# Six late skip terms seeded into PSUM by VectorE, with rows of x loaded into freed memory, and a new step list

## The chip, the cores and the metric

The kernel runs on one core of a Trainium2 chip. The metric is the device time of one execution in microseconds (us), taken as the median of several runs. A profile of one execution gives the spans and rows quoted here. The engines are named as the profile names them: PE (TensorE matmul), PEld (its weight loads), DVE (VectorE), ACT (ScalarE), POOL (GpSimd), and SP, whose queue issues most of the DMAs.

## The reference

The input x is 2048 x 512 in bfloat16. Two branches are computed from it and mixed by a gate.

```python
g = sigmoid((x * gate_w).sum(-1, keepdims=True))
# branch a: a diagonal complex state-space model and a skip term
Lam_bar = exp(dt * Lam);  B_bar = ((Lam_bar - 1) / Lam)[:, None] * Bmat
Bu = einsum("bld,pd->blp", x, B_bar)
h_t = Lam_bar * h_{t-1} + Bu_t                       # over 2048 rows
a = 2 * einsum("blp,dp->bld", hseq, Cmat).real + x * Dskip
# branch b: linear attention, 32 heads of 16, no causal mask
q, k, v = split(x @ wqkv)
phi(u) = concat(softmax(u @ w_phi), softmax(-(u @ w_phi)))
b = ((phi(q) @ kv) / (phi(q) @ z + 1e-6)) @ wo       # kv, z summed over all rows
out = g * a + (1 - g) * b
```

The change concerns the skip term `x * Dskip` of six of the sixteen output tiles.

## The kernel before, in words

The 2048 rows are handled as 16 tiles of 128 rows. Tile `ti` holds the rows with residue `ti // 2` modulo 8, in one half `ti % 2`, so that the recurrence can be run on eight residues with a scan over 128 blocks. The last stages run over the tiles in the order `order[n]`, n = 0 to 15.

All work of PE, DVE, ACT and the SP queue is put down in one hand-ordered string, `ORDER`. Each word of it is one step of a generator: `y8@6` advances the generator `st_y(8)` by one step and gives it PSUM bank 6, `o5:D` lets DVE do a copy that ACT would do otherwise, `t9:A` issues a DMA on ACT's queue in place of SP's. Every engine executes its own instructions strictly in the order in which the words stand, so an instruction that waits holds up all later ones of its engine.

The words that matter here:

- `F:34` issues 34 small matmuls without use (`spin`), ahead of the transposes `W0` to `W3` of the key weights and their folding `f0` to `f3`.
- `k`, `u`, `v` and `q` are the projections of a tile. `x`, `n`, `e` and `s` (capital letters behind the word `END`) are the feature maps: maximum, minimum, exponentials and normalisation of a group of four tiles. The last steps of `S1`, `S2` and `S3` multiply by a ratio on DVE (line 572) and issue four DMA transposes on SP (line 584), which give `phT`.
- `g`, `z`, `Z` and `h` are the state-space part, `c` the products that form the output matrices.
- `END` closes the memory pools of the first part and opens those of the second in their place.
- `y{n}` opens PSUM tile `py` with eight matmuls of 512 columns (line 754) and then adds the skip term by four matmuls of 128 columns against a diagonal matrix `Dd` (line 759).
- `o{n}` forms the attention numerators from `phT` (line 773), scales them on DVE into `on` (line 781) and transposes them into `oT`. For n = 0 to 11 that is a DMA transpose on SP (line 795), for the last four it is done by PE.
- `t{n}` adds four matmuls with `Wo` to the same `py` (line 802), scales by the gate (ACT line 806 or DVE line 808) and writes the rows out (line 810).

BT (transposes of B) and BD (the block matrix of the feature map) lie in the pool `pAC`, which is closed at `END`. `H_SEED` names eight `h` steps where ACT already writes a PSUM bank before matmuls accumulate onto it.

Of the kernel before, what the change touches and what calls it, by code (L numbers as in the profile page):

```python
# [25 lines left out]
R2 V@7 V U U f3@2 f3 P P P2 P2 P2 k0@4 V2@7 k3@1 P P2 P2 P2 P3 k0 V2 R5 P4 P4 P4 gw i3 k1@0 i1 i0 R3 k2@5 k1 k2 i0 i3  # L26
x0 u1@7 u1 Q1 P3 i3 v3@6 i1 i1 k3 i3:D u3@0 u3 i3 i1:D i1 v3 x0 u2@5 n0 n0 i0 x0 u0@7 x0 C0 u2 i0:D x0 i0 i2 n0 v2@2
x1 k5@4 k5 i2 v2 n0 x1 C6 u5@6 u5 i2 u0 i2:D i2 u4@0 k7@3 L k4@6 n0 U Q0 k4 C2 v4@7 k7 k6@1 k6 n1 u4:D n1 x1 Q2 v1@6
v1 e0 v5@5 e0 v7@0 k10@1 u7@4 v8@2 v5 n1 u8@6 Q3 u7 n1 v6@3 U v7 x1 x1 k10 v4 M v0@4 v0 n1 v6 x2 n2 k9@0 k9 k8@1 k8
u6@5 x2 n2 n2 u6 x2 s0 x2 n2 s0 s0 s0 s0 C3 s0 D k11@3 C4 e1 e1 k12@1 k12 C1 s0 k13@5 g40@7 k13 g00@0 g40 a0@15 a0 g00  # L30
s1 s1 C5 k11 u8 v8 C7 s1 s1 g10@7 g10 g10 g60@3 s1 g20@2 g60 x2 s1 k14@0 n2 k15@4 e2 e2 x3 g20 g30@7 s1 n3 a1 a1 g30
x3 n3 J0 e2 k14 J2 g30 e2 J1 x3 g50@2 g01@3 g50 g50 g01 n3 k15 x3 n3 g70@6 g70 g70 g62@2 x3 g70 n3 e3 g70 g11@4 g11 s2
g62 s2 s2 J3 g61@7 x4 s2 s2 s2 x4 g70:D g21@0 n4 g11 g41@6 x4 g21 g02@3 e3 e3 e3 g22@4 w2@0 w2 g22 s2 a2 g41 g51@2 g02
z0 z0 g61 n4 a2 z0 z0 a2 a2 u11@0 g31@4 n4 u11 z0 z0 n4 w0@6 w0 g31 g31 z0 s3 R7 w1@7 w1 g42@3 g42 z0 s3 x4 g51 g51 s3
s3 s3 z0 z0 Z0@7 s3 g71@0 w3@3 g71 v9@6 w3 q0@2 g71 g71 J2 J3 x4 n4 Z0 h50@3 e4 R6 h10@4 g71 g12@7 q0 g12 s3 h50 q3@2
h10 g71 a3 z1 g12 c4:D e4 e4 e4 h60@3 q3 z1 h60 g32@7 g32 q2@3 q2 g32 z1 v9 q1@4 q1 z1 u10@2 g52@0 g52 z1 z1 c2 g52 J1
g72@4 z1 g72 u10 c3 s4 z1 c5:D g72 g03@7 s4 nA c5 xA s4 g72 g72 g72 xA J0 v11@6 z1 z1 v12@0 s4 c5 nA v12 v13@3 s4 v11
v13 c2:D xA z2 u12@2 z2 u9@4 u9 c2 O v10@0 s4 u14@6 z2 v14@3 z2 z2 z2 u14 g03 g13@4 Z1@7 g13 xA v10 u15@6 c4 z2 g13
u15 nA z2 nA v14 c6:D z2 z2 a3 a3 a3 Z2@4 Z1 g23@0 c4 c6 h11@7 g23 Z2 c0 g33@6 xA nA c0 g33 g33 h52@0 c1 h51@4 u12 eA
h52 h11 g63@3 h12@6 g43@0 g43 g73@2 h62@0 g63 u13@7 g53@3 g53 h51 h61@4 s4 a4 eA eA h62 u13 v15@0 h12 h22@7 g53 eA c0  # L40
h61 h20@6 h22 sA h20 g73 v15 q10@3 a4 g73 h31@7 q10 g73 sA c1 g73 g73 a4 a4 Y h21@0 G q4@4 h31 h21 h31 G c1 q14@6 q14
q5@3 h30@0 Y q8@2 G c3 z3 z3 Y q5 z3 z3 h30 z3 z3 sA h30 z3 z3 c3 Y q8 q11@1 q11 sA sA z3 z3 q6@3 h41@0 sA h32@6 c6
q9@5 Z3@7 h33@1 Z3 q13@2 q4 h41 sA sA h32 q13 q9 sA h53@7 h53 h33 h33 sA h32 c7 q7@4 h13@2 h13 q6 q15@5 q7 q15 c7:D
h01@3 h63@0 h63 h02@0 sA h42@7 h42 c7 h03@5 h40@1 h23@6 h40 y6@2 h23 sA y2@4 h43@7 h01 h43 y6 h03 h00@1 h00 END h02
# [5 lines left out]
y11@1 E3 o8@2 S3 o8 o8@7 o8 o8 o8 o7 y11 S3 S3 o8 o9@2 o9 o9@7 o9 o9 y10 y12@2 o9 o9 y12 S3 t5:A S3 o11@7 S3 o11:D y12  # L50
y11 S3 S3 y10 o10@7 o10 t7 t7:D o11@7 o11 o11 o11 t8 t8:D S3 o11 S3 o10@7 o10 o10 S3@5 S3 o10 o10 t9 t9 S3@7 y15@3
S3:D o12@4 o12:D o12@7 t0 o14@5 o14:D y15 y15 o12 o12 t11 t1:A t11 o12 o14@4 o14 o12@5 o12:D y14@7 o13@5 o13:D t2
o13@1 o13:D o15@4 t8 o14 o14 t4 o13 t10 o15:D y14 o13 y14 o15@1 o14@4 t7:A t11:A o15:D o13@5 t12 o13:D t10 o15 t3 t13
t6:A t10 t12 t12 o15 o14:D t9:A o15@6 t14 t14 o15:D t13:D t13 t15 t15:D t15:A t14
# [18 lines left out]
def kernel(  # L73
# [667 lines left out]

    def phT_of(g):
        def make():
            live["ph", g] = pools["fq"][1].tile([P, 4, NB, P], BF16, name="phT")
            return lambda u: live["ph", g][:, u]
        return make

    def st_y(n):
# [8 lines left out]
        for kt in range(KT):
            xs = xT[:, kt, ti * P:(ti + 1) * P]
            MM(out=py[:, kt * P:(kt + 1) * P], lhsT=xs, rhs=Dd[:, kt, :], start=False, stop=False)
# [38 lines left out]
    def st_t(n):  # L798
        ti = order[n]
        py, oT = live["py", n], live["oT", n]  # L800
        for g in range(HG):
            MM(out=py[:], lhsT=oT[:, g, :], rhs=Wo[:, g, :], start=False, stop=(g == HG - 1))  # L802
        yield
        ot = pools["op"][1].tile([P, D], BF16, name="ot", bufs=14)
        if sel["eng"] == "act":
            nc.scalar.mul(out=ot[:], in_=py[:], mul=G[:, ti:ti + 1])  # L806
        else:
            VS(out=ot[:], in0=py[:], scalar1=G[:, ti:ti + 1], scalar2=None, op0=ALU.mult)
# [76 lines left out]
```

## Time and profile before

| | |
|---|---|
| median of 3 runs | 154.06 us (153.87 to 154.93) |
| profiled execution, its own time | 154.0 us |
| its span, first to last instruction | 151.9 us |
| time outside the span | 2.1 us |
| granted TensorE clock, mean | 0.995 |
| PE busy | 145.0 us, 95% |
| DVE busy | 136.1 us, 90% |
| ACT busy | 127.4 us, 84% |

PE busy includes the latency of pipelined matmuls. A group of four matmuls of 128 columns adds 0.22 us to PE's queue although the mean time of one is given as 219 ns; where PE is full, the distances between starts count. DVE and ACT rows likewise overlap their neighbours by about 0.1 us.

### The profile page before, as it was taken

The numbers are of one execution on the slowest core, as the hardware profiler recorded it, in microseconds if no ns is written. First come the engines' busy times: TensorE is split into PE (matmuls) and PEld (weight loads), VectorE is DVE, ScalarE is ACT, GpSimd is POOL, SyncE is SP. The second block draws the span as 40 slices with busy tenths as digits, with TensorE's granted clock in tenths as the row PEclk, the third lists the DMA queues.
The fourth block names the chain that finished last, engine by engine and source line by source line (L and its number), as shares of the span: only waits on it lengthen the run. The fifth ranks groups of instructions, "written<-read, shape, count | busy, mean of one in ns | idle before, by whom it ended". The sixth has DMA issues, their size and how long they took to land.

```text
span 151.9 us, 3442 instructions
## 1 busy us (share of the span) xinstructions
PE 145.0 (95%) x1251; PEld 99.9 (66%) x1268; DVE 136.1 (90%) x327; ACT 127.4 (84%) x305; POOL 14.7 (10%) x47
## 2 busy tenths in 40 slices
PE   7899999999999999999999999999999999999990
PEld 7647475778989976789887456655444655556640
DVE  3889999999999999999999999999999978874561
ACT  3389999999899999999999999989897759565550
POOL 8246880000000000000000000000000000000000
PEclk9999999999999999999999999999999999999998
DMA  3885997493454698830000003933076669747743
GB/s 104 178 209 81 201 206 152 96 99 85 97 103 100 123 208 175 173 125 4 0 0 4 2 0 76 134 70 69 0 107 140 139 138 155 160 105 172 245 142 104
DMA packets 48737, 17.03 MB, mean 112 GB/s; under 512 B 42064, under 2 KB 48720, under 8 KB 48720
## 3 DMA queue, kind: packets, MB, share of 16 engines
q1 hardware_dynamic: 47008, 15.36, 52.7%
...
q8 instruction: 10, 0.16, 0.5%
...
## 4 chain that ended last, share of the span: by engine, by line
PE 40%; SPq 30%; DVE 14%; DMA 10%; issue 3%; ACT 0%
SPq L236 13%; PE py L802 8%; PE pq L484 7%; PE py L754 7%; SPq L303 6%; DMA oT<-on 6%; PE pgq L619 6%; SPq L295 5%; PE pv L497 3%; SPq L299 3%; PE ph L705 3%; DMA X<-HM 2%; DMA HM<-in_A_C_im_dram 2%; DVE Bn L709 2%; DVE mxq L524 2%
## 5 line engine op out<-in xcount | busy, mean ns | idle before, releaser
L619 PE MATMUL pgq<-xT,BT 128*128 128x256 bf16 x256 | 31.8, 272 | 0.0
L619 PEld LDWEIGHTS <-BT 128*128 128x128 bf16 x256 | 24.7, 98 | 3.3
L143 ACT ACTIVATE EEk<-EEk 128x1024 bf16<-128x1024 bf16 x20 | 20.4, 1065 | 0.0
L484 PEld LDWEIGHTS <-xT 128*128 128x128 bf16 x128 | 12.1, 97 | 11.4 <-DMA xT<-in_A_x_dram 0.5
L124 ACT CAST uv<-pgq 128x512 bf16<-128x512 f32 x28 | 15.9, 594 | 1.1 <-PE pgq L626 0.6
L497 PE MATMUL pv<-Wv,xT 128*128 128x256 bf16 (+1 forms) x128 | 16.1, 272 | 0.0
L802 PE MATMUL py<-Wo,oT 128*128 128x512 bf16 x61 | 15.2, 379 | 0.5 <-DMA oT<-on 0.3
L484 PE MATMUL pq<-Wq,xT 128*128 128x512 bf16 x59 | 15.4, 378 | 0.3
L484 PE MATMUL pk<-Wk,xT 128*128 128x512 bf16 x60 | 15.2, 379 | 0.5 <-DMA xT<-in_A_x_dram 0.3
L497 PEld LDWEIGHTS <-xT 128*128 128x128 bf16 x128 | 12.2, 97 | 3.3 <-issue 0.5
L143 ACT ACTIVATE ld<-pn 128x16 f32<-128x16 f32 x32 | 5.8, 188 | 8.2 <-PE pn L773 7.7
L143 ACT ACTIVATE EEq<-EEq 128x1024 bf16<-128x1024 bf16 x12 | 11.9, 1049 | 0.2 <-DVE EEq L540 0.2
L124 ACT CAST vx<-pv 128x256 bf16<-128x256 f32 x31 | 11.7, 416 | 0.0
L124 ACT CAST Xq<-pk 128x512 bf16<-128x512 f32 x16 | 9.1, 597 | 0.5 <-PE pk L484 0.4
L802 PEld LDWEIGHTS <-oT 128*128 128x128 bf16 x64 | 5.6, 97 | 5.7 <-DMA oT<-on 0.7
L561 DVE TENSOR_TENSOR EEk<-EEk,rck 128x4096 bf16<-128x4096 bf16 (+1 forms) x5 | 9.3, 1857 | 0.0
L773 PEld LDWEIGHTS <-phT 128*128 128x128 bf16 x128 | 6.7, 97 | 3.8 <-issue 0.3
L124 ACT CAST Xq<-pq 128x512 bf16<-128x512 f32 x16 | 9.0, 604 | 0.0
L806 ACT ACTIVATE ot<-py,G 128x512 bf16<-128x512 f32 x9 | 6.2, 687 | 3.3 <-PE py L802 3.3
L524 DVE TENSOR_TENSOR smk<-smk 128x512 bf16<-128x512 bf16 (+4 forms) x18 | 8.1, 450 | 0.3
L608 ACT ACTIVATE phT<-X,dgB 128x512 bf16<-128x512 bf16 x11 | 8.2, 758 | 0.0
L124 ACT CAST nu<-pn 128x256 bf16<-128x256 f32 x22 | 8.1, 379 | 0.0
...
## 6 DMA issues: line engine op xcount, KB each, us to landing
X<-HM SPq DMA_DIRECT2D x8, 256.0 KB, 3.8
...
C2r<-in_B_wqkv_dram ACTq DMA_DIRECT2D x2, 256.0 KB, 3.6
...
```

Of the source, the lines that this page charges most:

```text
L124: nc.scalar.copy(out=out_ap, in_=in_ap)
L143: ins = nc.scalar.activation(**kw)
L236: nc.sync.dma_start_transpose(out=xT[:, :, ti * P:(ti + 1) * P], in_=x_res[ti // 2, ti % 2])
L303: nc.sync.dma_start_transpose(out=CA[:, ri, kt, :], in_=(A_C_re, A_C_im)[ri][:, kt * P:(kt + 1) * P])
L484: MM(out=pt[:], lhsT=xT[:, kt, ti * P:(ti + 1) * P], rhs=W[:, kt, :], start=(kt == 0), stop=(kt == KT - 1))
L497: MM(out=pv[:], lhsT=xT[:, kt, ti * P:(ti + 1) * P], rhs=Wvg[:, kt, c * hd:(c + 1) * hd + c], start=(kt == 0), stop=(kt == KT - 1))
L524: VT(out=dst, in0=cur[:, :, :, 0:n, :], in1=cur[:, :, :, n:2 * n, :], op=op)
L561: VT(out=E5, in0=E5, in1=rc.to_broadcast([P, L, 2 * NB, Dh, 4]), op=ALU.mult)
L608: nc.scalar.mul(out=t_, in_=x_, mul=c_)
L619: MM(out=pg[:, h, :], lhsT=BT[:, kt, 2 * j + h, :], rhs=xT[:, kt, r * NC:(r + 1) * NC], start=(h == 0 and kt == 0), stop=(r % 2 == 0 and k ...
L754: MM(out=py[:], lhsT=hs(r, t, slice(a * P, (a + 1) * P)), rhs=C2B[t], start=(t == 0), stop=False)
L802: MM(out=py[:], lhsT=oT[:, g, :], rhs=Wo[:, g, :], start=False, stop=(g == HG - 1))
```

## The change

For n = 8, 9, 10, 11, 13 and 15, `y{n}` has a new first step: DVE multiplies 128 rows of x, as they lie in memory, by Dskip laid over all partitions, and writes the product in float32 into the PSUM bank `py`. The eight matmuls then accumulate onto it, and the four matmuls against `Dd` are left out. For this, a new step `XN` issues five DMAs on SP: Dskip to 128 partitions (128 KB), and four loads of 256 KB with the rows of x of two tiles each. They go into the memory of BD and BT, which move to the pool `pBC` that stays open to the end. So the pools opened at `END` begin at other memory than before.

```diff
+Y_SEED = (8, 9, 10, 11, 13, 15)
...
-    BD = pAC.tile([P, HG, P], BF16, name="BD")
-    BT = pAC.tile([P, KT, NT2, P], BF16, name="BT")
+    BD = pBC.tile([P, HG, P], BF16, name="BD")
+    BT = pBC.tile([P, KT, NT2, P], BF16, name="BT")
+    xn = BT[:].rearrange("p k t c -> p (k t c)").rearrange("p (n d) -> p n d", n=8)
+    Db = BD[:].rearrange("p k f -> p (k f)")
...
+    def st_XN():
+        nc.sync.dma_start(out=Db, in_=A_Dskip.unsqueeze(0).to_broadcast([P, D]))
+        yield
+        for h in range(4):
+            ti = order[8 + 2 * h]
...
+            nc.sync.dma_start(out=xn[:, 2 * h:2 * h + 2, :], in_=x2.rearrange("(c a r) d -> r c a d", r=NR, c=P)[ti // 2])
+            yield
...
+        if n in Y_SEED:
+            VT(out=py[:], in0=xn[:, n - 8, :], in1=Db, op=ALU.mult)
+            yield
         for t in range(NT2):
-            MM(out=py[:], lhsT=hs(r, t, slice(a * P, (a + 1) * P)), rhs=C2B[t], start=(t == 0), stop=False)
+            MM(out=py[:], lhsT=hs(r, t, slice(a * P, (a + 1) * P)), rhs=C2B[t], start=(t == 0 and n not in Y_SEED), stop=False, skip_group_check=n in Y_SEED)
             if t % 4 == 3:
                 yield
+        if n in Y_SEED:
+            return
         for kt in range(KT):
             xs = xT[:, kt, ti * P:(ti + 1) * P]
```

The step list is new as a whole. What of it the prediction speaks of: the first words, and the stretch in which `S1` ends.

```diff
-B NI l10 l8 F:34 W0@1 W0:D W1@7 W1:D l9 W2@5 W2:D NR W3@2 W3 l11 l12 l13 l14 R0 R1 f0@3 f0:D l15 f1@1 f1 R4 f2@5 f2:D
+NI B l8 NR l12 F:54 W0@5 W0:D l9 W1@4 W1 W3@0 W2@3 W2 W3:D l10 l11 f0@6 f0:D f1@4 f1 f3@5 f3:D l13 f2@2 f2 V@7 V U U P P
...
-S1 N2 S1 o3 S1 q12 t0 y1@0 o1 S1 o3 S1 o1 N2 t0 S1 y8 S1 S1 S1 S1 E2 E2 y9@4 y1 y9 X3 t3 X3 X3 N3 E2 E2 X3 t3 X3 S2 y1
+XN N2 X2 y1@3 y1 y1 N2 X2 S1 o3 XN S1 o3 N2 S1 o1 o1 t0 S1 t0 N2 S1 S1 S1 y4@7 y8@6 S1 S1 S1 S1 X3 S1 y13@5 X3 E2 E2
+y9@2 X3 N3 y8 y8 E2 E2 X3 X3 S2 t3 t3 t3:A t1 t1 y9 o4@4 y13 o4 o4@3 o4 y9 o4 o4 o5@4 o5 o5@3 o5 o5 y13 S2 S2 o6@4 o6
```

The copies change hands too. Ahead of `END`, DVE gives one of its three `W` copies, the copy of `u4` and, on balance, one half product of `c` to ACT. Behind `END` it gives away the copies in `o5`, `o6`, `o7`, `o11`, `o13`, `o14` and `o15` and two scalings (`t8`, `t13`), and takes over one in `o12` and `o14` each, the scaling of `t12` and the copy of one `phT`. Five output DMAs move from SP to ACT's queue and three the other way.

More of the change, by code (lines that the diff above doesn't have):

```diff
@@ L24 @@
 ORDER = """
-B NI l10 l8 F:34 W0@1 W0:D W1@7 W1:D l9 W2@5 W2:D NR W3@2 W3 l11 l12 l13 l14 R0 R1 f0@3 f0:D l15 f1@1 f1 R4 f2@5 f2:D
[L26 to L44, printed above, removed]
@@ L45 @@
-o0@6 X1 h01 h03 y6 h00 y2 N1 o0 o0@1 y5@6 h02 o0 o2@3 o2 o2@1 o2 o2 o0 y2 y5 o1@1 o3@3 y3@5 y3 y3 X1 N1 o1 X1 y0@1 y0
-y0 N1 X1 N1 X1 N1 E1 y5 E1 E1 X2 o2 o2 X2 E1 o1@0 o1 t2 o3 o3@0 o3 N2 o0 o0 X2 o3 q12@7 N2 X2 N2 X2 S1 o1 y8@3 G t2 S1
-S1 N2 S1 o3 S1 q12 t0 y1@0 o1 S1 o3 S1 o1 N2 t0 S1 y8 S1 S1 S1 S1 E2 E2 y9@4 y1 y9 X3 t3 X3 X3 N3 E2 E2 X3 t3 X3 S2 y1
-t1 y4@1 t1 o4@7 o4 o4@5 o4 S2 N3 S2 y13@0 o4 o4 y9 S2 o5@5 o5 o5@7 y8 o5:D o5 o5 S2 S2 y4 o4 N3 o6@7 o6:D o6@5 N3 o6
-y4 y13 o6 o6 o5 o6 S2 S2 S2 y7@5 y7 y7 o7@7 S2 S2 S2 y13 o7 N3 t4 t4:D t5 t5:D o7@7 E3 E3 o7:D E3 t6 y10@6 t6:D o7 o7
@@ L50 @@
[L50 to L54, printed above, removed]
+NI B l8 NR l12 F:54 W0@5 W0:D l9 W1@4 W1 W3@0 W2@3 W2 W3:D l10 l11 f0@6 f0:D f1@4 f1 f3@5 f3:D l13 f2@2 f2 V@7 V U P P
@@ new lines @@
+P R0 P2 P2 P2 P2 U k0@3 k0 R1 V2@0 P2 k1@4 P4 P4 P4 l14 R2 P3 l15 P3 V2 k1 i3 i1 i0 P2 gw i0 i3 i3 i3:D i3 i0 R3 n0
+i0:D i0 k2@2 k2 i1 i1 R5 x0 k3@3 k3 n0 n0 i2 x0 x0 i2 v3@4 v3 u1@6 R4 u1 u2@7 u2 u4@0 u4 v2@5 x0 u5@2 i2 i1:D i1 U v2
+i2:D i2 Q1 k5@1 x0 x1 k5 n0 u3@7 u5 x1 x1 L C0 u3 k7@4 k7 u0@0 u0 k4@1 k4 k6@2 n0 n1 n1 C2 v5@5 x1 u6@3 k6 v7@6 v5 C6
+v1@1 u6 C4 v7 e0 v0@0 v0 U v4@5 M v6@7 n1 v6 e0 v8@4 n1 x1 n1 u7@3 u7 n2 k8@6 k8 k12@7 x2 Q0 v4 k9@6 D k10@0 e1 v1 e1
+k11@1 x2 s0 s0 x2 k13@5 s0 s0 n2 Q2 s0 s1 k10 s0 g40@2 s1 s0 k13 s1 k12 x2 s1 n2 g40 k9 g20@3 g20 a0@72 v8 k11 a0
@@ new lines @@
+g00@0 k14@3 g00 s1 s1 n2 x2 n2 n3 Q3 k14 u8@4 s1 g10@0 g10 x3 x3 u8 g10 k15@1 e2 e2 g30@3 a1 J0 g30 g30 n3 k15 a1
+g50@4 g50 g01@1 x3 e2 e2 g60@5 n3 g50 x3 C7 n3 x3 n3 e3 n4 u11@0 s2 g60 x4 g62@3 s2 g01 g70@4 g70 g02@5 g62 u11 g70
+g70 e3 g70 g41@3 n4 u10@1 g21@6 C1 s2 x4 s2 x4 g02 s2 s2 g70:D g41 n4 C3 g11@0 g11 g22@4 C5 e3 e3 g11 z0 g22 g61@5 n4
+z0 g51@3 x4 z0 z0 z0 g61 z0 J1 w1@0 w1 u10 s2 g21 a2 a2 J2 w0@4 z0 a2 a2 s3 s3 z0 g31@1 g31 s3 w0 s3 s3 s3 g31 w2@5 w2
+z0 z0 g42@0 x4 w3@6 w3 g51 n4 g51 g42 Z0@5 Z0 J2 g71@1 g71 g71 q0@6 h50@0 g71 s3 e4 h10@3 h10 g71 g71 z1 z1 q0 h50
@@ new lines @@
+v9@4 v9 J3 g12@5 a3 g12 g12 J3 q1@1 e4 e4 R6 h60@4 z1 v10@3 e4 v10 q1 z1 z1 z1 h60 q2@0 q2 q3@4 v12@5 z1 q3 z1 c2:D z1
+z1 s4 c5:D g32@6 g32 g32 Z1@3 c3 v12 s4 Z1 g52@1 g52 g52 c4 R7 h11@3 g72@4 J1 xA c5 s4 s4 s4 g72 g72 g03@5 g03 J0
+u14@6 xA nA xA g72 g72 g72 s4 c2:D nA v14@0 v14 u9@5 c2 u9 O h11 g23@1 g23 c4 c5 g13@3 g13 g13 nA z2 nA z2 z2 z2 z2
+u14 v13@4 v11@1 v11 z2 v13 u15@0 xA z2 z2 a3 c4 z2 c0 c6 c0 u15 h51@6 a3 a3 z2 Z2@3 h51 Z2 g43@4 g33@5 g43 u13@3 xA c1
+h52@0 nA h52 c1 c1 g33 c0 g63@6 g33 u13 s4 h61@0 h61 h62@4 g53@5 g63 h12@6 u12@3 eA g53 h62 eA u12 h12 g73@1 v15@3 g53
@@ new lines @@
+eA h20@5 g73 h20 h21@4 v15 G a4 a4 h22@0 g73 c6 g73 h21 eA h22 a4 a4 Y q5@3 c6 G h31@5 Y g73 g73 sA h30@4 q6@0 h31 h31
+q5 Y q6 sA z3 z3 Y q14@7 q10@1 q10 h30 h30 q8@6 q8 sA z3 z3 z3 z3 sA sA h32@0 z3 h41@2 q14 z3 h41 sA sA q9@1 z3 z3
+q13@5 q9 sA sA sA q11@3 h32 q13 G q11 c3 h40@4 Z3@2 Z3 h40 h32 h33@7 sA q4@1 q4 q7@3 q7 c3 h53@5 h53 h42@2 h42 h13@6
+h13 h33 h33 c7 c7:D q15@0 h63@5 h63 y6@1 c7 h00@2 q15 h43@6 h43 sA h01@5 h03@0 h23@3 h02@7 y6 y6 h01 h01 y2@6 h02 h02
+h03 h03 h00 h00 h23 END o0@3 o0 y2 o0@4 o0 y2 o2@7 o2 o2@0 X1 o2 o2 o0 N1 XN X1 o1@2 N1 o1 X1 N1 X1 y0@5 y0 y0 N1 X1
@@ new lines @@
+N1 y3@4 o2 o0 X2 E1 E1 q12@2 y3 o3@3 E1 E1 XN o2 o0 y5@0 o3 o3@7 o3 y5 y5 t2 G o3 o1@7 XN X2 q12 N2 t0 o1 o1 y3 X2 t2
+XN N2 X2 y1@3 y1 y1 N2 X2 S1 o3 XN S1 o3 N2 S1 o1 o1 t0 S1 t0 N2 S1 S1 S1 y4@7 y8@6 S1 S1 S1 S1 X3 S1 y13@5 X3 E2 E2
+y9@2 X3 N3 y8 y8 E2 E2 X3 X3 S2 t3 t3 t3:A t1 t1 y9 o4@4 y13 o4 o4@3 o4 y9 o4 o4 o5@4 o5 o5@3 o5 o5 y13 S2 S2 o6@4 o6
+o5 o4 o5 o6@3 o6 o6 S2 N3 o6 y4 o6 S2 S2 S2 N3 N3 S2 S2 S2 y7@4 S2 S2 N3 o7@3 y7 y7 o7 y4 o7@3 t4 t4:D t1:A t5 y11@7
+o7 o7 o7 o7 E3 t5:D t6 t6:D y11 y11 y10@0 E3 E3 E3 S3 o8@1 o8 o8@3 o8 o8 o8 o8 t4:A S3 y10 y10 o9@1 S3 o9 t5:A y12@3
@@ L55 @@
+o9@1 o9 o9 S3 o9 S3 S3 y12 o11@1 o11 S3 S3 o9 S3 S3 y12 o10@1 o10 t7 o11@1 o11 o11 t7:D t8 t8 o11 y15@6 S3@1 o10@4
+S3:D o10 o10 t9 o10 o11 t9 S3@4 y15 o12@1 t2:A o14@2 S3:D o12 o14 y15 o14@1 o14:D o12@4 o12:D o10 t8 o12 o12 o14 y14@2
+o13@1 o13:D y14 o13@4 o14 o13:D o15@1 o15:D t11 y14 o12@1 o12:D o13 t11 o15@4 o15 t10 o15 t7 o13 o15 t6:A t10 o14@1
+o13@4 t11 o13 o14:D t12 t12:D o15@7 t14 t13 o15 t12:A t14 t13 t13:A t10 t9 t15 t15:D t15:A t14
 """
@@ L740, in st_END @@
         yield
+    def st_XN():
[3 more added lines that the diff above has]
+            ti = order[8 + 2 * h]
+            for a in range(2):
+                assert order[8 + 2 * h + a] == ti + a
+            nc.sync.dma_start(out=xn[:, 2 * h:2 * h + 2, :], in_=x2.rearrange("(c a r) d -> r c a d", r=NR, c=P)[ti // 2])
+            yield
     def phT_of(g):
@@ L801, in st_t @@
         for g in range(HG):
-            MM(out=py[:], lhsT=oT[:, g, :], rhs=Wo[:, g, :], start=False, stop=(g == HG - 1))
+            MM(out=py[:], lhsT=oT[:, g, :], rhs=Wo[:, g, :], start=False, stop=(g == HG - 1), skip_group_check=n in Y_SEED)
         yield
@@ L815 @@
     st = {"V": st_V(), "V2": st_V2(), "U": st_U(), "P": st_P(), "P2": st_P2(), "P3": st_P3(), "P4": st_P4(), "B": st_B(), "gw": st_gw(),
-          "M": st_M(), "D": st_D(), "L": st_L(), "G": st_G(), "Y": st_Y(), "END": st_END(), **{f"Z{j}": st_Z(j) for j in range(4)}, "NR": st_N(0), "NI": st_N(1), "O": st_O()}
+          "M": st_M(), "D": st_D(), "L": st_L(), "G": st_G(), "Y": st_Y(), "END": st_END(), **{f"Z{j}": st_Z(j) for j in range(4)}, "XN": st_XN(), "NR": st_N(0), "NI": st_N(1), "O": st_O()}
     for n in range(8, NTI):
```

## The prediction

> **What bounds the kernel now.** I read the page's busy times first, then a table of busy time by stretch, then PE's and SP's lists of waits, then the order of time around the waits that were left.
>
> ```profile
> PE 145.0 (95%) x1251; PEld 99.9 (66%) x1268; DVE 136.1 (90%) x327; ACT 127.4 (84%) x305; POOL 14.7 (10%) x47
> ```
> ```profile
> core 0: us, PE busy (x) PEld busy (x) DVE busy (x) ACT busy (x) POOL busy (x), PEclk, DMA share, GB/s
> 1.11:9.40 8.29, 7.81 (x76) 5.94 (x78) 5.91 (x32) 4.24 (x7) 4.23 (x13) 1.00 0.71 165
> 9.40:97.20 87.80, 87.04 (x770) 65.91 (x777) 86.40 (x209) 85.63 (x197) 9.95 (x30) 1.00 0.54 102
> 97.20:115.00 17.80, 17.69 (x129) 9.58 (x129) 17.66 (x37) 16.31 (x38) 0.00 (x0) 1.00 0.45 58
> 115.00:123.00 8.00, 7.85 (x72) 4.50 (x72) 7.59 (x16) 4.67 (x17) 0.00 (x0) 1.00 0.67 144
> 123.00:133.30 10.30, 9.86 (x85) 5.45 (x85) 8.27 (x15) 7.97 (x23) 0.00 (x0) 1.00 0.84 154
> 133.30:148.30 15.00, 14.76 (x129) 8.48 (x132) 9.35 (x22) 8.56 (x27) 0.00 (x0) 1.00 0.60 168
> ```
>
> PE is full: between 1.11 and 148.3 it is idle for 0.48 + 0.76 + 0.11 + 0.15 + 0.44 + 0.24 = 2.18 us. But up to 115 us DVE is just as full (86.40 of 87.80, 17.66 of 17.80), and to 97 us ACT too (85.63 of 87.80). DVE has room only from 123 us on. So PE is the bound, with DVE hardly behind it until the end of S2, and an order of steps that is a little worse for DVE shows in PE.
>
> ```profile
> PE spin L849 <- DVE fillw L162: 1.1, 1, 1.1
> PE pvt L317 <- DMA vec_n<-in_A_log_dt_dram: 0.4, 1, 0.4
> PE py L802 <- DMA oT<-on: 0.3, 1, 0.3
> PE pk L484 <- DMA xT<-in_A_x_dram: 0.3, 1, 0.3
> ```
> ```profile
> L759 PE MATMUL py<-Dd,xT 128*128 128x128 bf16 x64 | 5.6, 219 | 0.0
> 121.26 1.22 DVE L572 TENSOR_TENSOR EEq<-EEq,rhoq 128x2048 bf16<-128x2048 bf16 x1
> 119.12 3.81 SPq L795 DMA_TRANSPOSE oT<-on  x3
> 123.03 5.66 SPq L584 DMA_TRANSPOSE phT<-EEq  x4
> 128.78 5.13 SPq L795 DMA_TRANSPOSE oT<-on  x3
> 131.81 0.83 PE L759 MATMUL py<-Dd,xT 128*128 128x128 bf16 x12
> 132.71 0.29 PE L773 MATMUL pn<-KVm,phT 128*128 128x68 bf16 x4
> 133.26 1.04 PE L802 MATMUL py<-Wo,oT 128*128 128x512 bf16 x4 [0.27 <-DMA oT<-on]
> 148.26 0.75 DVE L808 TENSOR_SCALAR ot<-py,G 128x512 bf16<-128x512 f32 x1 [0.64 <-PE py L802]
> ```
>
> The one late wait of PE, at 133.26, is t7's. By the step list the row at 131.81 is the skip terms of y12, y11 and y10, then comes o10, then t7. t7 needs the oT of o7, which SP issued at 128.78, behind the four phT transposes of S2 (123.03, for 5.66 us). These follow S2's last product on DVE (121.26 + 1.22 = 122.48) and the three oT before them (119.12 + 3.81 = 122.93). So there is a chain DVE, SP, DMA, t7, whose end PE meets with almost nothing to spare. Behind it PE works until 148.26, the last scaling starts, and the span ends at 151.9.
>
> **The change part by part.** The sum is made against the profiled execution's 154.0 us (span 151.9 and 2.1 around it); the runs' median is 154.06, so no correction is needed.
>
> *Skip matmuls removed.* Twelve take 0.83 us, with 219 ns for the last alone: (0.83 - 0.22) / 11 = 0.055 us each. Six tiles of four: 24 x 0.055 = 1.3 us less on PE. But five of the six tiles (8, 9, 10, 11, 13) have their skip term ahead of t7 in the old list. PE's 1.1 us there only makes the wait at t7 longer unless the chain that feeds t7 comes earlier as well. What surely remains is y15's 0.2 us, **-0.2**, and the rest decides between cases.
>
> *Twenty more spins.*
>
> ```profile
> 1.11:3.76 2.65, 2.65 (x26) 2.65 (x27) 1.00 0.55 143
> 3.76:4.43 0.67, 0.67 (x11) 0.50 (x9) 1.00 1.13 341
> ```
> ```profile
> 4.37 1.25 PE L281 MATMUL ptw<-ident,C2r 128*128 128x128 bf16 x16
> 6.74 0.16 PE L317 MATMUL pvt<-ident,vec_n 12*128 12x12 bf16 x1 [0.39 <-DMA vec_n<-in_A_log_dt_dram]
> 15.77 0.60 PE L484 MATMUL pk<-Wk,xT 128*128 128x512 bf16 x2 [0.26 <-DMA xT<-in_A_x_dram]
> 4.81 1.09 DVE L126 COPY Xq<-ptw 128x512 bf16<-128x512 bf16 x3
> ```
>
> The first spins come every 2.65 / 26 = 0.10 us, and from 3.76 on at the pace of 0.055. Twenty more cost 20 x 0.055 = 1.1 us: W0 starts at 5.5 instead of 4.37, and DVE's first copy at 5.9 instead of 4.81. PE gets back its waits at 6.74 (0.39) and 15.77 (0.26). On DVE I take +1.1 less the idle that it has there (8.29 - 5.91 = 2.4 up to 9.4, part of it before 4.81): I take 0.4 as absorbed. **+0.7**, bounds 0 and 1.1. The granted clock column shows 1.00 although PE stands idle up to 0.4 us at 6.74, and the pace of the spins doubles at 3.76, inside the old 34. The Trainium skill (TensorE: Matmul & The Clock Gate, What's actually happening) says that the clock opens after one busy window of about 3.4 us and closes after an idle one of that length. By it the added spins win nothing, and the term stays at its cost; were the clock lost without them, it would be 0.
>
> *Six seeds on DVE.* No row shows a product of two bf16 operands written to PSUM.
>
> ```profile
> L781 DVE TENSOR_TENSOR on<-nu,rd 128x512 bf16<-128x512 bf16 x16 | 6.7, 422 | 0.8 <-ACT rd L143 0.4
> L709 DVE TENSOR_TENSOR Bn<-ph,uv 128x512 bf16<-128x512 f32 x8 | 5.4, 685 | 0.1
> L124 ACT CAST ph<-uv 128x512 f32<-128x512 bf16 x8 | 4.6, 638 | 0.0
> L126 DVE CAST vx<-pv 128x256 bf16<-128x256 f32 x1 | 0.4, 415 | 0.0
> L126 DVE CAST nu<-pn 128x256 bf16<-128x256 f32 x10 | 4.0, 421 | 2.1 <-ACT ld L143 1.9
> L610 DVE TENSOR_SCALAR phT<-X,dgB 128x512 bf16<-128x512 bf16 x5 | 1.7, 347 | 0.0
> ```
>
> The bounds are 0.42 us (same shapes, all in SBUF) and 0.69 us (one float32 operand in PSUM); ACT's write of the same float32 tile to PSUM takes 0.64, so I take 0.69. The Trainium skill (VectorE: DVE Perf Modes, The perf-mode tier table) gives a two-tensor operation with any operand in PSUM half the rate of one in SBUF; by it the value is the upper one, without it three seeds would cost 1.3 instead of 2.1. Three seeds (y8, y13, y9) stand on DVE ahead of S2's first step, y8's directly ahead of S1's last product: 3 x 0.69 = **+2.1** on the chain to t7 (bound 1.3). Those of y11, y10 and y15 stand where DVE is idle (8.27 of 10.30, 9.35 of 15.00): 0, and if that cover were gone 0.7 each.
>
> *Copies given to ACT.* Ahead of S2's end DVE loses one W copy (1.09 / 3 = 0.36), u4's (0.41), half a product of c (0.35) and the copies in o5 and o6 (2 x 0.42): **-2.0**. ACT's share of this up to END is 1.1 to 1.2 us on an engine that has 2.2 us idle in 87.80, so the bound the other way is that DVE waits for ACT by as much: -0.8. Finally DVE's idle time between 115 and 123 (0.41) can take up **-0.4** (bound 0).
>
> *The five loads.*
>
> ```profile
> 96.31 2.32 SPq L584 DMA_TRANSPOSE phT<-EEk  x1
> 103.09 8.81 SPq L795 DMA_TRANSPOSE oT<-on  x4
> SPq L795 <- DVE on L781: 7.5, 4, 4.3
> 56.55 1.26 SPq L308 DMA_DIRECT2D X<-HM  x2
> X<-HM SPq DMA_DIRECT2D x8, 256.0 KB, 3.8
> 110.96 1.22 DVE L572 TENSOR_TENSOR EEq<-EEq,rhoq 128x2048 bf16<-128x2048 bf16 x1
> ```
>
> An issue on SP takes 1.26 / 2 = 0.63 us, five 3.2. The new list puts two of them behind the four phT transposes that end at 96.31 + 2.32 = 98.63, ahead of the first oT at 103.09, and three among the next oT, where SP again stands waiting for `on` (7.5 us in four waits, 4.3 the longest). Cost **0**; without this cover o3's and o1's transposes would move by up to 1.9. A load of 256 KB landed 3.8 us after its issue, so the first tiles' rows are there by about 104, and y8's seed comes on DVE only just ahead of S1's last product, which began at 110.96: 0 as well.
>
> *The rest.* One output DMA, t0's, now stands on SP ahead of S1's transposes, but t0 is scaled before DVE has S1's last product: 0, at most one issue, 0.6. The other pool addresses make writers behind `END` wait for other readers, all of which stand well ahead in the list: 0. The tail behind the last matmul (scaling on DVE, DMA on ACT's queue) is the same: 0.
>
> *Sum.* The chain to t7 moves by 0.7 + 2.1 - 2.0 - 0.4 = +0.4, PE behind it gives -0.2: 154.0 + 0.2 = **154.2 us**, no change to be told from the runs. I take 1% of the median, 1.5 us, as what a measurement of this kernel tells from no change: 152.5 to 155.6.
>
> **The rivals.**
>
> *PE stays the bound.* If the new list brings oT of o7 earlier, as a list made for this change may, t7 does not wait, and the skip terms count in full: -1.3 + 1.1 for the spins, less the waits at 6.74, 15.77 and 133.26 (0.39 + 0.26 + 0.27 = 0.9): 154.0 - 1.1 = 152.9. For it speaks that behind 123 us DVE and ACT have room; against it, that three seeds are put ahead of S2 on an engine that is full there.
>
> *Faster: the idle time goes too.* PE's whole idle is 2.18 us in many small pieces. If the list takes out three quarters of them (1.6), the time is 154.0 - 1.3 + 1.1 - 1.6 = 152.2, and 151.6 if all go. Against it: 0.76 of them are spread over 87.8 us.
>
> *Slower: ACT gives nothing back, and DVE's seeds fall on the chain in full.* ACT is idle for 2.17 of 87.80 us up to 97, and it starts later by the spins too. If the W, u4 and c copies that it takes over come back as waits of DVE for ACT (-1.2 lost), and the early idle takes up nothing, the chain moves by 1.1 + 2.1 - 0.8 - 0 = 2.4: S1's last product and with it S2, the oT of o4 to o7 and t7 come late, PE stands at o4 and at t7, and the time is 154.0 - 0.2 + 2.4 = 156.2. It is slower by over 1% from a chain that is 1.7 us late. For it speaks that y8's seed stands in front of S1's last product, with the four phT transposes of S1 queued behind it on SP and o4 to o7 behind these; against it, that ACT has room from 97 us on (16.31 of 17.80, then 4.67 of 8.00).
>
> **How the numbers follow.** The forecast, 154.2, has 0.34, with a range of its own from 153.4 (seed 0.42) to 155.2 (half of ACT's share lost, nothing absorbed between 115 and 123). PE as the bound, 152.9, has 0.18, so within 1% has 0.52. The idle time gone, 152.2, has 0.18 for faster by over 1%. The seeds in full, 156.2, have 0.30 for slower by over 1%: more than faster, since three engines are full at once and every part added lies on the one that feeds t7. The range from 152.0 to 156.3 takes in all four and leaves out the far end of either rival.
>
> **What would show it.** In the profile after: spins over about 5.4 us and W0 at 5.5; 40 skip matmuls in place of 64; six DVE products at 0.6 to 0.7 us each; SP's last phT issue of S2 at 128.7 or up to 0.8 later; a wait of t7's PE for oT of 0.5 us or more, though the skip terms ahead of it are gone. Wrong would be: no wait of PE at the late t steps (then the gain is near 1.1), DVE waiting for ACT by more than 1 us ahead of S1's end (then the slow rival), or a seed that waits for its bank or its load.

## The result, and the profile after

The changed kernel takes 155.17 us in the median (154.44 to 156.33, 18 runs) against 154.56 us (153.31 to 155.51, 18 runs) for the kernel before on the same chip: a ratio of 1.0049, with a 95% interval of 1.0025 to 1.0073. It is slower by 0.6 to 0.8 us, which is inside the 1% that the prediction called no change, and 1.0 us above its 154.2. The 1.3 us of matmuls that the change takes from PE show nowhere in the time. Ratios here and below are those on record, formed from the fast executions alone, without those more than 1.5% above the fastest of their kernel; they differ from the quotient of the two medians by up to 0.2%, or 0.3 us.

One caution on all that follows. The profiled execution after took 156.33 us and is the slowest of its 18, that of before took 154.0. Executions of one and the same kernel lie up to 2.2 us apart, so the traces are compared by stage, and only the medians of many runs decide.

The busy times of the page and the table by stretch follow, in the order in which the prediction reads them for the kernel before. In this trace the last matmul ends 2.4 us later than in before's (150.61 against 148.22), so the two late stretches are taken 2.4 us later, to hold about the same work:

```profile
PE 147.3 (95%) x1250; PEld 101.1 (65%) x1264; DVE 135.9 (88%) x323; ACT 130.6 (85%) x315; POOL 14.3 (9%) x47
```
```profile
1.11:9.40 8.29, 8.29 (x88) 7.87 (x89) 3.89 (x19) 3.04 (x5) 3.55 (x9) 1.00 0.73 160
9.40:97.20 87.80, 86.81 (x764) 65.09 (x770) 85.16 (x213) 85.06 (x196) 10.27 (x33) 1.00 0.54 99
...
125.40:135.70 10.30, 9.54 (x67) 4.47 (x65) 8.83 (x16) 8.02 (x23) 0.00 (x0) 1.00 0.92 177
135.70:150.70 15.00, 14.64 (x126) 8.23 (x127) 9.18 (x20) 10.07 (x30) 0.00 (x0) 1.00 0.50 135
```

The columns after the stretch's length are the busy times of PE, PEld, DVE, ACT and POOL. Two things differ from before. In the stretch that began at 123, DVE had 2.03 us of room (8.27 of 10.30) and now has 1.47 (8.83). And PE, which was idle for 0.44 us there, is idle for 0.76. The groups that the change touches, and rows of the order of time on PE, come next. In the second row BT and BD are the names of the memory in which the rows of x and Dskip now lie:

```profile
L867 PE MATMUL spin<-fillw 128*128 128x128 bf16 x54 | 5.9, 314 | 1.1 <-DVE fillw L163 1.1
L767 DVE TENSOR_TENSOR py<-BT,BD 128x512 f32<-128x512 bf16 x6 | 4.2, 696 | 0.7 <-ACT ot L824 0.7
L777 PE MATMUL py<-Dd,xT 128*128 128x128 bf16 x40 | 3.7, 219 | 0.0
```
```profile
3.75 3.30 PE L867 MATMUL spin<-fillw 128*128 128x128 bf16 x29
6.85 1.20 PE L284 MATMUL ptw<-ident,C2r 128*128 128x128 bf16 x16
9.21 1.23 PE L487 MATMUL pk<-Wk,xT 128*128 128x512 bf16 x4
101.01 0.29 PE L791 MATMUL pn<-KVm,phT 128*128 128x68 bf16 x4
147.86 2.75 PE L820 MATMUL py<-Wo,oT 128*128 128x512 bf16 x12
```

The change does what it says: 40 skip matmuls in place of 64, and six products on DVE of 0.70 us each. The spins are another matter. From 3.75 to 6.85 there are 29, one every 0.107 us. In before's trace they came at 0.055 from 3.76 on. In this execution PE did not come up to speed before W0, so W0 starts at 6.85, 2.5 us later than the 4.37 before, and the first projection at 9.21. These are the same rows of before:

```profile
7.07 1.21 PE L484 MATMUL pk<-Wk,xT 128*128 128x512 bf16 x4
97.88 0.29 PE L773 MATMUL pn<-KVm,phT 128*128 128x68 bf16 x4
146.55 1.67 PE L802 MATMUL py<-Wo,oT 128*128 128x512 bf16 x7
```

From the first projection to the first numerators (`pn`) it is 97.88 - 7.07 = 90.81 us before and 101.01 - 9.21 = 91.80 after. From there to the end of the last matmul it is 148.22 - 97.88 = 50.34 before and 150.61 - 101.01 = 49.60 after. A little of the 1.0 us lost in the first stretch is work that only moved: y6's skip term (four matmuls, 0.22 us) and the copies of `h00` to `h03` stood behind the first `o0` and now stand ahead of it. Together the two stretches take 141.15 us before and 141.40 after. So this trace's loss is in the start, and behind the first projection the saved 1.3 us are gone from the length. Behind the first numerators 0.74 us are won, and some of what is missing there stands in new late waits, 0.64 us where before had 0.27:

```profile
135.13 0.29 PE L791 MATMUL pn<-KVm,phT 128*128 128x68 bf16 x4 [0.31 <-ACT nu L125]
135.59 1.04 PE L820 MATMUL py<-Wo,oT 128*128 128x512 bf16 x4 [0.17 <-DMA oT<-on]
...
136.91 1.04 PE L820 MATMUL py<-Wo,oT 128*128 128x512 bf16 x4 [0.16 <-DMA oT<-on]
```

By the step list these are o10, t7, o11 (left out) and t8. The next rows, from the chain that ended last, say what they wait for:

```profile
124.33 1.14 DVE EEq L575
125.46 1.15 DVE EEq L543
...
126.63 3.01 ACT EEq L144 x4
129.65 3.91 DMA phT<-EEq
133.55 3.31 DMA oT<-on
...
136.91 1.04 PE py L820 x4
```

Here the chain, as the profile infers it, runs from DVE's last product of S2 (line 575) over the exponentials of the next group, the last phT transpose of S2 and o8's oT to t8. In before the same stretch of the chain ran on PE, up to its step aside for o7's oT. What sets the start of t8 is now DVE, ACT and the transposes, and PE arrives early.

### The profile page after: what moved, and what is told of

Read it like the earlier page. It is cut to its first block, busy times and chain, and to the rows that moved or that the text cites. A ratio compares the mean times of both kernels' runs of the same rounds, so it can differ in the third digit from the quotient of the medians.

```text
span 154.5 us, 3470 instructions
## 1 busy us (share of the span) xinstructions
PE 147.3 (95%) x1250; PEld 101.1 (65%) x1264; DVE 135.9 (88%) x323; ACT 130.6 (85%) x315; POOL 14.3 (9%) x47
## 4 chain that ended last, share of the span: by engine, by line
DVE 36%; ACT 27%; PE 24%; DMA 7%; issue 3%; SPq 0%; DVEq 0%; ACTq 0%
PE py L770 8%; ACT Xq L125 6%; DVE smk L527 6%; PE py L820 5%; DMA phT<-EEq 4%; PE spin L867 4%; ACT phT L611 4%; DVE EEk L564 4%; ACT vx L125 3%; ACT uv L125 3%; DVE mxk L527 3%; ACT EEk L144 2%; DVE mnk L527 2%; DMA oT<-on 2%; ACT EEq L144 2%
## 5 line engine op out<-in xcount | busy, mean ns | idle before, releaser
L144 ACT ACTIVATE EEk<-EEk 128x1024 bf16<-128x1024 bf16 x20 | 21.6, 1118 | 0.0
L125 ACT CAST uv<-pgq 128x512 bf16<-128x512 f32 x28 | 16.5, 613 | 0.4 <-PE pgq L627 0.4
L500 PE MATMUL pv<-Wv,xT 128*128 128x257 bf16 (+1 forms) x128 | 16.7, 272 | 0.1
L125 ACT CAST vx<-pv 128x256 bf16<-128x256 f32 x32 | 12.8, 435 | 0.0
L144 ACT ACTIVATE ld<-pn 128x16 f32<-128x16 f32 x32 | 6.3, 200 | 6.9 <-PE pn L791 6.7
L125 ACT CAST nu<-pn 128x256 bf16<-128x256 f32 x27 | 10.0, 391 | 0.0
L611 ACT ACTIVATE phT<-X,dgB 128x512 bf16<-128x512 bf16 x12 | 8.8, 789 | 0.0
L791 PE MATMUL pn<-KVm,phT 128*128 128x68 bf16 x128 | 8.0, 194 | 0.5 <-ACT nu L125 0.3
L824 ACT ACTIVATE ot<-py,G 128x512 bf16<-128x512 f32 x10 | 6.7, 687 | 1.9 <-PE py L820 1.1
```

The source lines that it names most:

```text
L125: nc.scalar.copy(out=out_ap, in_=in_ap)
L144: ins = nc.scalar.activation(**kw)
L500: MM(out=pv[:], lhsT=xT[:, kt, ti * P:(ti + 1) * P], rhs=Wvg[:, kt, c * hd:(c + 1) * hd + c], start=(kt == 0), stop=(kt == KT - 1))
L611: nc.scalar.mul(out=t_, in_=x_, mul=c_)
L791: MM(out=pn[:, 4 * m:4 * m + 4, :].rearrange("p h e -> p (h e)"), lhsT=ph[:, 4 * hf + m, :], rhs=KVm[:, 4 * hf + m, :], start=(m == 0), st ...
```

## The experiments

The first four ran on one chip, beside 154.65 us for before. Ratios are against before on the same chip throughout.

**Spins alone, in either list.**

```diff
-NI B l8 NR l12 F:54 W0@5 W0:D ...
+NI B l8 NR l12 F:34 W0@5 W0:D ...
```

> The changed kernel with 34 spins in place of 54, all else as changed. Theory (the spins pay the bill): the 20 extra spins stand on PE ahead of everything, 20 x 0.055 = 1.1 us at the fast pace and 20 x 0.107 = 2.1 us where the clock opens late, as in the profile after; so this is 1.1 to 2.1 us faster than the changed kernel, 153.1 to 154.1, and 0.5 to 1.4 faster than before. Rival (the chain over DVE to t7): the later start is absorbed in early waits and the seeds ahead of S2 set the end; then at most 0.4 us faster than the changed kernel, about 154.8 to 155.2.

Measured: 154.81 us, ratio 1.0016 (0.9989 to 1.0043). The other way round, before with `F:54` in place of `F:34`:

> The kernel before with 54 spins in place of 34, all else as before. Theory (the spins pay the bill): PE is full in this list, so the end moves by the spins less the early waits at 6.74 and 15.77 us, +0.5 to +1.8 us: 155.1 to 156.4. Rival (start absorbed): within 0.4 us of before, 154.2 to 155.0.

Measured: 154.96 us, ratio 1.0023 (0.9995 to 1.0051). Twenty spins cost 0.0023 x 154.65 = 0.36 us in the old list, and (1.0049 - 1.0016) x 154.6 = 0.5 in the new one. Neither figure is told from zero by itself (the first lies between 0.1 less and 0.8 more, and the second compares two chips), but they agree. By these values the spins are half to two thirds of the whole loss. Single traces show more. In the old list with 54 spins the first projection and the last matmuls are these:

```profile
7.97 1.21 PE L484 MATMUL pk<-Wk,xT 128*128 128x512 bf16 x4
147.26 1.89 PE L802 MATMUL py<-Wo,oT 128*128 128x512 bf16 x8
```

Both come 0.9 us later than before's: 7.97 against 7.07 (6.99 and 7.01 in two other traces of the old list with 34 spins), and an end at 149.15 against 148.22. So in this execution nothing of the delay is absorbed behind the first projection. In the traces of the new list, 54 spins in place of 34 put the first projection 1.64 us later (9.21 against 7.57) and the end of the last matmul 1.84 (150.61 against 148.77). Why the medians show less is not known. The profiled executions of the three kernels with the new list and 54 spins, in which W0 stood at 6.64 to 6.85, were each 1.0 to 1.2 us slower than the median of their kernel, so these traces overstate what the spins cost.

By the medians the first run leaves the new list with 34 spins 0.25 us over before (between 0.2 under and 0.7 over), still without the 1.3 us. Both times lie in the range of the rival, the start absorbed, though the trace above shows no absorption behind the first projection.

**No seed at all, in the new list.** The skip terms of all tiles go back to PE, as the last step of each `y`, and the loads go.

```diff
-Y_SEED = (8, 9, 10, 11, 13, 15)
+Y_SEED = ()
...
-XN
```

> The changed step list with the skip terms of all sixteen tiles on PE again: no seeds, no loads of rows of x or of Dskip. Each seed step is taken out of the list, and the skip matmuls stand right behind the second half of y. PE has 1.3 us more to do, DVE 6 x 0.69 = 4.2 us less, SP five issues less. Theory (the spins pay the bill, the seeds win their matmuls): +0.8 to +1.3 us against the changed kernel, about 156.0 to 156.5. Rival (the seeds' DVE time lies on the chain to t7): DVE is freed by 2.1 us ahead of S2, which is worth as much as the matmuls or more: 0.8 us faster to equal, 154.4 to 155.2.

Measured: 155.68 us, ratio 1.0065 (1.0033 to 1.0098). Six seeds against 24 skip matmuls are worth (1.0065 - 1.0049) x 154.6 = 0.25 us, with intervals that overlap, so a gain is not told from a small cost. In the two traces the stretch from the first projection to the end of the last matmul is 0.68 us shorter with the seeds (141.40 against 142.08). Why three products of 0.7 us ahead of S2 do not put S2 back is seen in DVE's waits between 97 and 134 us, of this kernel and then of after:

```profile
DVE smq L535 <- ACT EEq L152: 1.7, 1, 1.7
DVE on L807 <- ACT rd L152: 1.6, 2, 1.3
DVE EEq L583 <- ACT rhoq L152: 0.4, 1, 0.4
```
```profile
DVE smq L527 <- ACT EEq L144: 0.3, 1, 0.3
```

and in SP's order of time, of this kernel and then of after:

```profile
125.90 5.89 SPq L595 DMA_TRANSPOSE phT<-EEq  x4
131.88 4.25 SPq L821 DMA_TRANSPOSE oT<-on  x3
```
```profile
125.62 5.29 SPq L587 DMA_TRANSPOSE phT<-EEq  x4
131.01 5.39 SPq L813 DMA_TRANSPOSE oT<-on  x3
```

Without the seeds DVE stands waiting for ACT for 3.7 us, with them for 0.3. S2's transposes go out no earlier without the seeds: they start 117.05 us behind the first projection (125.90 - 8.85), against 116.41 with them (125.62 - 9.21). The new list has put the products where DVE would wait.

**Three seeds.** Only the late ones are left, those of y8, y9 and y13 are skip terms on PE again.

```diff
-Y_SEED = (8, 9, 10, 11, 13, 15)
+Y_SEED = (10, 11, 15)
```

> The changed step list with seeds for three tiles only, n = 10, 11 and 15, the ones on DVE behind S2; y8, y9 and y13 have their skip matmuls on PE again, right behind the second half of y. PE has 0.66 us more to do than the changed kernel, DVE 2.1 us less ahead of S2. Theory (the seeds win their matmuls): +0.3 to +0.7 us against the changed kernel, 155.5 to 155.9. Rival (the three seeds lie on the chain to t7): 0.5 to 1.5 us faster than the changed kernel, 153.7 to 154.7.

Measured: 156.31 us, ratio 1.0123 (1.0071 to 1.0175). It is slower than with six seeds (1.0025 to 1.0073); against none the intervals overlap widely. Neither theory foresaw this. In its chain t7 is reached over an oT that took 5.11 us to land:

```profile
131.75 5.11 DMA oT<-on
```

Before's slowest took 4.44. But in the changed kernel with six seeds one oT took 5.4 us, so a slow transpose does not by itself explain the time. This result stays unexplained.

**The two halves of the list, exchanged.** The next four ran beside 154.19 us for before. By the traces so far the early part of the new list cost time and the late part won some, so the parts were joined crosswise at `END`.

> The list of before up to END with its 34 spins, and the list of after behind END, with the five loads and the six seeds; four pool banks are renamed so that the two halves meet. The profiles so far put the loss of the new list ahead of END: W0 to the first projection took 94.2 to 94.7 us in kernels with the new list and 93.0 to 93.5 with the old, and the stretch from there to the last matmul 49.0 to 49.2 with the new list and its seeds against 50.0 with the old. Theory (the halves add): the time is that of before less 0.6 to 0.9, near 153.8, ratio 0.994 to 0.996, PE's wait at t7 about 0.5. Rival (the halves belong together: the late part needs the lead that the early part of the new list gives DVE and ACT): no gain, 154.5 to 155.2, with S1's last product and oT of o7 at least 0.5 us later than in after, measured from the first projection.

Measured: 156.54 us, ratio 1.0138 (1.0093 to 1.0183). The join itself was at fault, as PE's list of waits shows:

```profile
PE py L779 <- DVE Bn L721: 1.7, 1, 1.7
```

y6 had been given the bank of h40, which an addition on DVE (line 721) was still reading. The other mix:

> The list of after up to END, with 34 spins, and the list of before behind END; no loads, no seeds, all skip terms on PE. Theory (the early part of the new list costs by itself, 0.3 to 0.6 by the profiles): 154.9 to 155.4, ratio 1.002 to 1.006. Rival (the early part is what helps, since it hands copies from DVE to ACT ahead of S1, and the seeds spend it): 153.8 to 154.4, with S1's first product earlier against W0 by 0.5 to 1.5.

Measured: 155.82 us, ratio 1.0089 (1.0054 to 1.0124). In its trace PE waits for 0.27 us at the first numerators behind the join, and two later `t` steps wait for oT, 0.30 us at 126.05 and 0.90 at 135.82. It is slower than either theory said; why was not followed up, and nothing is taken from it. The first mix was run again with the banks of its late part renamed as a whole, on a third chip beside 154.24 us for before:

```diff
-y6@1 ... y2@6 ... h00@2 ... END ... o0@3 o0 y2 o0@4
+y6@2 ... y2@4 ... h00@1 ... END ... o0@6 o0 y2 o0@7
```

> Once more the list of before up to END and the list of after behind it, now with the pool banks of the late part renamed as a whole, so that each bank's last user ahead of END is the same step as in before: in the first mix y6 had to wait 1.8 us for a bank that a copy of W still held, and all behind it was late by that. Theory (the halves add, and the early part of the new list is what costs): 0.4 to 0.9 under before, ratio 0.994 to 0.997. Rival (the gain of the late part needs the early part of the new list): within 0.3 of before or slower, ratio 0.998 to 1.006, with PE's late waits for oT at 0.8 us or more.

Measured: 154.60 us, ratio 1.0018 (0.9988 to 1.0049). The theory, 0.994 to 0.997, falls: leaving out the early part of the new list does not bring the gain. The profiled execution took 153.42 us, and it was the fastest of twelve. Its stages alone would have told a gain that the median does not have.

**What PE's 1.3 us are worth.** Before, with the six skip terms left out:

```diff
+            if n not in (8, 9, 10, 11, 13, 15):
-            MM(out=py[:, kt * P:(kt + 1) * P], lhsT=xs, rhs=Dd[:, kt, :], start=False, stop=False)
+                MM(out=py[:, kt * P:(kt + 1) * P], lhsT=xs, rhs=Dd[:, kt, :], start=False, stop=False)
```

> Before with the skip term of tiles 8, 9, 10, 11, 13 and 15 left out altogether, 24 matmuls and nothing in their place: that part of the computation is missing, and the time is what the change could win at most in the old list if DVE did the skip terms for nothing. Theory (t7 waits for oT, which hangs on DVE and SP, so what PE saves ahead of t7 comes back as a longer wait there): 0 to -0.5 us, ratio 0.997 to 1.000, PE's wait at t7 grows to 0.9 or more. Rival (PE's time is the bound): -1.0 to -1.3, ratio 0.992 to 0.9935, and the waits stay as they are.

Measured: 153.83 us, ratio 0.9977 (0.9953 to 1.0001), that is 0.36 us less, between 0.72 less and nothing. This is the run that decides. Even free of charge, taking the matmuls away wins at most about half of their time in the old list. PE's waits behind the spins are these:

```profile
PE pk L484 <- DMA xT<-in_A_x_dram: 0.8, 1, 0.8
PE pn L774 <- DVE nu L126: 0.5, 1, 0.5
PE py L803 <- DMA oT<-on: 0.3, 1, 0.3
```

The first stands at 16.30 us, far ahead of all that was left out, and so belongs to this execution (before had 0.26 there). The other two are o10's `pn`, just ahead of t7, and t8. At t7 itself, where the theory wanted 0.9, there is none. These late waits add up to 0.83 us where before had 0.27: 0.56 of the 1.3 us come back as waits. The other 0.76, a little more than the medians allow, are won in this trace, in which the first `pn` to the end of the last matmul takes 49.58 us against 50.34 (two other traces of the old list have 50.12 and 50.37).

**Two output DMAs out of the way.**

> After with 34 spins, and the output DMAs of t4 and t5, which go out at 131 to 132 us on ACT's queue beside the transposes of o7, put on SP's queue behind t8 in the list. In after an oT transpose lands 2.9 us after its issue (2.4 in before, where nearly all output DMAs come behind 138). Theory (these transfers hold up the transposes): the wait of PE at t7 to t9 shrinks, -0.3 to -0.8 us against the new list with 34 spins (154.81), so 154.0 to 154.5. Rival (the transposes are late because on is late, not for the transfers): 0 against 154.81, the landing time of oT unchanged within 0.1.

Measured: 154.88 us, ratio 1.0035 (1.0008 to 1.0061), against 1.0016 for the new list with 34 spins. There is no gain, PE's wait for oT in its trace is 1.0 us, and oT lands 2.5 us after its issue in the median, against 2.4 in the new list with 34 spins. These transfers are not what holds the transposes up.

**o7 transposed on PE.** Beside 154.24 us for before:

```diff
-OT_PE = (12, 13, 14, 15)
+OT_PE = (7, 12, 13, 14, 15)
...
-o7 o7 o7 o7 E3 t5:D t6 t6:D y11 y11 y10@0
+o7 o7 o7 E3 t5:D t6 t6:D y11 o7@3 y11 o7:D y10@0
```

> After with 34 spins, and o7 transposed by four PE matmuls and a copy on DVE in place of SP's DMA transpose. In the new list with 34 spins on of o7 was ready at 126.69, its oT was issued at 129.37 behind the four phT transposes of S2, those of o8 and o9 at 130.71 and 132.97 behind it, and t9 waited 0.6 us for the last. Theory (SP's order of transposes sets the late t steps): o8 is issued 0.5 to 1.3 us earlier, PE's waits at t7 to t9 go, -0.6 net of 0.22 us of PE work, so 0.3 to 0.8 under the 154.81 of the new list with 34 spins, ratio to before 0.9965 to 0.9995. Rival (PE stays the bound, or the waits only move to the next bank or tile): 0 to +0.3 against it, ratio 1.001 to 1.004.

Measured: 154.81 us, ratio 1.0025 (0.9994 to 1.0056): no gain over 1.0016. The wait for oT left the list of PE's waits as the theory said, but t9 starts at 136.46 us, where it stood at 136.52 with o7 on SP: PE only comes to it later. One late wait is new:

```profile
PE py L779 <- DVE py L776: 0.2, 1, 0.2
```

o8's oT was issued at 130.70, as late as the 130.71 with o7 in front of it, because `on` of o8 was not ready. SP's order was not the last link. DVE stands ahead of it, and the order of time on DVE in the new list with 34 spins shows how:

```profile
124.88 0.74 DVE L826 TENSOR_SCALAR ot<-py,G 128x512 bf16<-128x512 f32 x1
125.66 0.70 DVE L767 TENSOR_TENSOR py<-BT,BD 128x512 f32<-128x512 bf16 x1
126.27 0.42 DVE L799 TENSOR_TENSOR on<-nu,rd 128x512 bf16<-128x512 bf16 x1
126.60 1.40 DVE L826 TENSOR_SCALAR ot<-py,G 128x512 bf16<-128x512 f32 x2
127.92 0.69 DVE L767 TENSOR_TENSOR py<-BT,BD 128x512 f32<-128x512 bf16 x1
128.93 1.23 DVE L527 TENSOR_TENSOR smq<-EEq 128x2048 bf16<-128x2048 bf16 x1 [0.32 <-ACT EEq L144]
130.07 0.42 DVE L799 TENSOR_TENSOR on<-nu,rd 128x512 bf16<-128x512 bf16 x1
```

The seeds of y11 and y10 (line 767) stand among the scalings of t4 to t6, with hardly a gap. `on` of o8, at 130.07, follows S3's first sum, which itself waits 0.32 us for ACT's exponentials. In the chain of this run y10's seed is a link, on the way over o9 to the transpose that t9 waits for:

```profile
128.00 0.62 DVE py L767
...
128.66 1.89 PE py L770 x8
...
132.97 3.50 DMA oT<-on
```

With o7 on PE, the wait above, 0.2 us, is that of PE for y10's seed itself (line 776 there).

**The loads alone, in the old list.** `Y_SEED = ()`, five words `XN` put in behind `END`, BD and BT in the memory of the change:

> Before's list with the five loads of x and Dskip put into it, BD and BT in the memory of the change, and no seed: the rows are loaded and not used. Theory (the loads stand where SP waits anyway, and 1.1 MB more between 97 and 118 us meets no one): 0, ratio 0.998 to 1.002, oT of o0 to o3 issued within 0.2 of before. Rival (the loads, or the memory that they now share, hold up the transposes of S1 or of the first oT): +0.5 to +1.0, ratio 1.003 to 1.0065, S1's first phT issue 0.5 us or more later against the first projection.

Measured: 154.22 us beside 154.24, ratio 1.0016 (0.9982 to 1.0049). SP's order of time holds the loads where it stood waiting:

```profile
98.92 0.62 SPq L761 DMA_DIRECT2D BT<-in_A_x_dram  x1
103.17 2.52 SPq L822 DMA_TRANSPOSE oT<-on  x2
...
112.60 5.95 SPq L596 DMA_TRANSPOSE phT<-EEq  x4
```

The first oT goes out at 103.17 (103.09 before), and S1's first phT at 112.60 (112.21 before) in an execution whose first `pn` came 0.24 later. No cost of the loads is told; the interval reaches 0.75 us.

**All remedies at once.** The mix with matched banks, 34 spins, and o7 on PE, beside 154.50 us for before:

> The mix of the two lists (before up to END, after behind it, banks matched) with o7 transposed on PE as well: each of the three things that the traces named as eating the gain (spins, the early part of the new list, the wait of the t steps for oT) is out. By the profiles the stretch from the first projection to the last matmul took 49.96 us in before, 49.31 in the mix and 48.79 in the new list with o7 on PE. Theory (these were the costs, and the profiles can be added): 0.8 to 1.2 under before, ratio 0.992 to 0.995. Rival (neither PE nor the oT chain alone sets the end; what is gained at one place is given back between executions and at the next wait, as in the mix and in the new list with o7 on PE, whose medians stood at 1.002 and 1.0025): ratio 0.997 to 1.004.

Measured: 154.78 us, ratio 0.9997 (0.9967 to 1.0028). It is before's time, not 0.8 us under it. In its trace a single wait for o9's oT takes 1.00 us, where the mix without o7 on PE had 0.66. No version was found that beats both kernels.

## Why the prediction was right, and where it was not

**No change: right. The step that carried it holds by half.** That step was that 1.1 of the 1.3 us taken from PE only lengthen waits of the late `t` steps. The run with the skip terms left out bears it out in kind: 0.36 us won (0 to 0.72), 0.2 forecast. In its trace 0.56 us come back as late waits, half of what was forecast. The rival that PE stays the bound, with 152.9, is refuted by that run and by the result, and so is the one at 152.2.

**Spins, +0.7 forecast: not contradicted.** The runs give 0.36 and 0.5, with intervals that take in 0.7. W0 was forecast for 5.5 and stood at 6.85, because the time at which PE comes up to speed was taken from one trace as if it were fixed. The Trainium skill's rule (TensorE: Matmul & The Clock Gate, What's actually happening) that the clock opens after a busy window of about 3.4 us would put W0 at 5.7, an estimate from that figure and the two paces, and does not give this execution's 6.85 either.

**Seeds, 0.69 each: right. +2.1 on the chain: wrong.** So was **-2.0 for the copies given to ACT**. The two were costed as if DVE were full throughout. In the new list DVE had become the one that waits for ACT, by 3.7 us between 97 and 134 when the seeds are out. The reading is that the copies given away came back as waits and the seeds filled them; no run gave the copies back, so it is argued from the waits and not shown. The two errors, +2.1 and -2.0, cancel, and that the sum came out near the result is in good part luck. The transposes of S2 are a check on it: the last phT issue stood 120.0 us behind the first projection before (127.09 - 7.07) and 120.4 in the new list with 34 spins (128.01 - 7.57). The step sums had put it 0.3 earlier without the spins' share. The slower rival, 156.2, needed the seeds to fall on the chain in full, and the run without seeds refutes that. Its other half, that what ACT is given comes back, fits the waits. The sign that the prediction named for it, DVE waiting for ACT by more than 1 us ahead of S1's end, is there in a smaller size, 0.7 us (below).

**Late seeds at 0, since DVE is idle behind 123: partly wrong.** The idle time of a stretch was not where the seeds fell. The scalings of t4 to t6 and the seeds of y11 and y10 stand side by side, the seed of y10 lies on the chain of the new list with 34 spins, and that of y15 waits 0.7 us for ACT to read its bank, which the prediction had named as a sign of error.

**The wait at t7: the cause was too narrow.** Instead of 0.5 us or more at t7, PE waits 0.31, 0.17 and 0.16 at o10, t7 and t8, and with 34 spins 0.6 at t9. Relieving SP for t7 brings no gain, since the next `on` is late on DVE.

**Loads at 0: not contradicted** (ratio 0.9982 to 1.0049).

**What stays open.** Of the loss of 0.6 to 0.8 us, the spins explain 0.4 to 0.5, with intervals from nothing to all of it. The chain that ended last differs at the start: in before it stands on SP's loads and transposes of the inputs and on the DMAs behind them up to 54.66 us, and not on PE; in the old list with 54 spins it begins on the spins. How much of the spins counts may differ with that. That the six seeds win 0.25 is not told from zero; if so, the new order of steps itself costs some 0.5 to 0.65 (1.0065 without seeds, less the spins' 0.0023 to 0.0033), and the exchange of the halves did not locate it. One wait that before does not have stands in every trace with the early part of the new list, at 22.45 us in the changed kernel:

```profile
DVE mnk L527 <- ACT Xq L125: 0.7, 1, 0.7
```

In these seven traces the first projection to the first `pn` takes 91.8 to 92.0 us, and in those of the old list 90.8 to 91.2. But the mix with the old early part, which lacks the wait, has no better median (1.0018 against 1.0016), so it is not shown to be the cause. The 156.31 of three seeds is not understood.
